# Holding the input loads of later batches until the batch ahead is turned, with a rearranged first batch and a split last tile

## The chip, the cores and the metric

The kernel runs on one core of one Trainium2 chip. The metric is the device time of one execution in microseconds (us), the median over several executions. A profile shows one execution alone: the kernel before took 443.82 us in its profiled run, and its span, from the first to the last of the program's instructions, is 442.0 us. Engines are named as the profile names them: PE is TensorE's matmuls, PEld its weight loads, DVE is VectorE, ACT is ScalarE, POOL is GpSimd, SP is SyncE. A trailing q (SPq) is the engine's queue of instructions that issue transfers.

Two kernels are compared by the ratio of mean times: the mean of one kernel's fast runs over the mean of the other's in the same rounds, so a ratio is not quite the ratio of the medians quoted beside it.

## The reference, cut to what matters

```python
batch, n_q_heads, n_kv_heads, seq, head_dim = (8, 16, 4, 384, 64)

def _attn_ref(q, k, v):                       # grouped-query attention
    k = np.repeat(k, 4, axis=1); v = np.repeat(v, 4, axis=1)
    scores = np.matmul(q, k.transpose(0, 1, 3, 2)) / np.sqrt(64)
    attn = np.exp(scores - scores.max(-1, keepdims=True))
    attn = attn / (attn.sum(-1, keepdims=True) + 1e-09)
    return np.matmul(attn, v)

def _moe_ref(x, w_in, w_out):                 # x: 3072 x 1024
    h = np.maximum(x @ w_in, 0.0)             # 1024 x 2048, "up"
    return h * h @ w_out                      # 2048 x 1024, "down"
```

Inputs and output are float32; the kernel computes in bfloat16.

## The kernel before: the parts that matter

One batch at a time goes through: load k, q, v (GpSimd issues the transfers, which also cast to bfloat16); *turn* k and q, that is transpose them so that the head dimension lies on the partitions; scores; exponential; attention times values; turn the result; up; down; store. Batches 0 and 1 are turned by TensorE. From batch 2 on, three transposing transfers issued by SyncE do it, one for k and one for each half of q.

```python
NST, NEX, NXT, NHR, NY = 2, 8, 3, 4, 3      # two staging buffers for k, q, v

def load_k(b):
    st = b % NST
    R.add("gpsimd", lambda g: g.dma_start(k_st[st]..., k[b]...),
          writes=[("k_st", st)], dma=f"k{st}", cost=1.3, issue=0.8)

def turn_q_dma(b, half):                    # SyncE
    R.add("sync", lambda e: e.dma_start_transpose(out=qT[b % 2][...], in_=q_st[b % NST][...]),
          reads=[("q_st", ...)], writes=[("qT", ...)], dma=f"turn_q{half}", cost=2.5)

# ... cut: at the start, in this order on GpSimd's queue: batch 0, three chunks of w_in,
#     batch 1, five chunks of w_in, four chunks of w_out ...
```

The order of instructions on every engine is fixed when the program is built. A planner keeps a modelled clock for each engine, and at each step appends to TensorE's order the piece of work that its model says is ready. The hardware then runs that order:

```python
while av_q or sc_q or o_q or f_head is not None:
    if loaded + 1 < B and turned >= loaded + 1 - NST and not turn_q:
        loaded += 1
        load_k(loaded)
        load_q(loaded, 0, 8)
        load_q(loaded, 8, 16)
        load_v(loaded)
    # ... cut: queue the turns of the next batch; list what is ready; append one piece to TensorE ...
```

With `turned` starting at 1 and `NST` at 2, the loads of batches 2 and 3 are both issued as soon as batch 1 is turned. In the first batch the kernel before swaps two half tiles:

```python
items = list(ffn(b))
if b == 0:
    items[1], items[2] = items[2], items[1]
```

The softmax here doesn't subtract the row's maximum and nothing guards it: scores larger than these inputs give would overflow.

## Time and profile before

| | before |
|---|---|
| median of 3 runs | 444.37 us (444.08 to 444.77) |
| span of the profile | 442.0 us |
| PE busy | 423.0 us, 96% |
| PE idle in one stall | 77.15 to 86.90 us |

The page of the kernel before: busy times, then three rows of the span in 40 slices of 11.05 us. A digit is tenths busy; PEclk is the granted TensorE clock in tenths.

```profile
PE 423.0 (96%) x3438; PEld 230.2 (52%) x3438; DVE 159.0 (36%) x333; ACT 193.1 (44%) x189; POOL 55.1 (12%) x68
...
PE   7799999199999999999999999999999999999997
...
PEclk9999999699999999999999999999999999999999
DMA  9999999999589359448017220023100110110011
```

PE is full but for the first slices, the last one and one slice that reads 1, at 77 to 88 us. That slice also has the only lowered clock. The transfer engines are full through the first 110 us.

The timeline of the kernel before around that slice. Columns: start, duration, engine, line, operation, out<-in, shape, count; the bracket is the idle time of the engine before it and what ended it.

```profile
64.04 13.11 PE L450 MATMUL ps<-w_out_sb,h2T 128*128 128x512 bf16 x60
...
69.66 3.21 SPq L263 DMA_TRANSPOSE kT<-k_dup  x1
...
72.91 11.62 SPq L269 DMA_TRANSPOSE qT<-q_st  x2
...
86.90 1.46 PE L342 MATMUL ps<-qT,kT 64*128 64x512 bf16 x8 [9.75 <-DMA qT<-q_st]
...
88.30 2.83 PE L450 MATMUL ps<-w_out_sb,h2T 128*128 128x512 bf16 x8
```

PE runs 60 down matmuls of batch 0 to 77.15, then waits 9.75 us for the first query turn of batch 2. Work for PE exists in that time (eight down matmuls, the up matmuls of batch 1), but in the fixed order it stands behind the scores.

The table by stretches of the kernel before. Columns: length and PE busy (count), the same for PEld, DVE, ACT and POOL, then granted clock, transfer share (the packets' summed time over that of 16 engines; it can pass 1, as packets overlap), GB/s.

```profile
75.00:80.00 5.00, 2.15 (x10) 0.78 (x8) 0.69 (x1) 0.00 (x0) 0.28 (x1) 1.00 1.39 178
80.00:85.00 5.00, 0.00 (x0) 0.00 (x0) 0.00 (x0) 0.00 (x0) 0.00 (x0) 0.50 1.39 179
85.00:90.00 5.00, 3.10 (x13) 1.04 (x14) 0.00 (x0) 1.59 (x1) 2.18 (x3) 0.50 1.19 218
```

PE does nothing from 80 to 85, the transfer engines are no less busy, and the clock is at half, so the first work after the wait runs at half speed too.

GpSimd's timeline in the kernel before, the loads of batches 2 and 3 (k, two halves of q, v, twice; the first k of each and the last v are shown), and what waited for the first ones:

```profile
30.84 0.79 POOL L202 DMA_DIRECT2D k_st<-in_k_dram  x1
...
34.07 0.81 POOL L202 DMA_DIRECT2D k_st<-in_k_dram  x1
...
36.55 0.84 POOL L220 DMA_DIRECT2D v_st<-in_v_dram  x1
65.89 1.47 POOL L254 COPY k_dup<-k_st 128x1536 bf16<-128x1536 bf16 x1 [28.49 <-DMA k_st<-in_k_dram]
73.76 0.83 POOL L259 COPY v_aug<-v_st 128x768 bf16<-128x768 bf16 x1 [6.41 <-DMA v_st<-in_v_dram]
```

Batch 2's first piece lands at 65.8 and its last at 73.7, because both weight matrices, 8.4 MB each in float32, are ahead of it in the queue. Batch 3 follows in the same queue; by the trace's record of landings its four pieces land at 76.0, 79.7, 83.4 and 85.3, just while the turns of batch 2 run.

How long the first query turn took from issue to landing, in the kernel before, for batch 2 (issued at 72.91) and for batch 4 (issued at 127.11, nothing loading beside it):

```profile
DMA to landing us min/median/max: 13.9/13.9/13.9
```

```profile
DMA to landing us min/median/max: 3.9/3.9/3.9
```

ScalarE's first chain of exponentials and up work of batch 0, in the kernel before:

```profile
7.28 16.61 ACT L332 ACTIVATE expT<-ps 128x1024 bf16<-128x1024 f32 x18 [4.79 <-PE ps L322]
...
21.52 0.82 PE L422 MATMUL ps<-xT,w_in_sb 128*128 128x384 bf16 x4
...
23.29 0.81 PE L422 MATMUL ps<-xT,w_in_sb 128*128 128x384 bf16 x4
```

The last copy of the kernel before, and (transfers of the last 8 us) the time from issue to landing of the stores there:

```profile
438.85 0.69 DVE L462 COPY y_sb<-ps 128x512 f32<-128x512 f32 x1 [2.76 <-PE ps L450]
```

```profile
out_dram<-y_sb SPq DMA_DIRECT2D x2, 256.0 KB, 2.0
```

### The profile page before, as it was taken

To read this page: it belongs to the slowest core of one execution; us is meant where nothing else is said; L and a number is where in the kernel's file an instruction comes from. 1 tells how busy PE (TensorE), PEld (TensorE's weight loads), DVE (VectorE), ACT (ScalarE), POOL (GpSimd) and SP (SyncE) were. 2 spreads that over 40 slices of the span, in tenths; PEclk is the share of its full clock that TensorE was granted. 3 is DMA by queue.
4 is the path that set the end of the run, shared out by engine and by line. 5 is a ranking of instruction groups with operands and counts; after the bars stand their busy time and mean duration, and the time that the engine had idled before them with its cause. 6 is when DMAs were issued, how large, how long until landed. Compare 5 with 4: busy or idle time off the path is not lost.

```text
span 442.0 us, 7776 instructions
## 1 busy us (share of the span) xinstructions
PE 423.0 (96%) x3438; PEld 230.2 (52%) x3438; DVE 159.0 (36%) x333; ACT 193.1 (44%) x189; POOL 55.1 (12%) x68
## 2 busy tenths in 40 slices
PE   7799999199999999999999999999999999999997
PEld 4465554055644556445564455555565456446543
DVE  4374441034423445223452334343342234124411
ACT  4937730067743676545755457722131023003300
POOL 7763002043022013020000000000000000000000
PEclk9999999699999999999999999999999999999999
DMA  9999999999589359448017220023100110110011
GB/s 148 194 196 203 183 193 213 196 160 171 72 160 192 76 101 139 82 91 165 19 37 150 78 78 19 1 62 99 57 0 25 71 49 0 50 71 25 1 73 71
DMA packets 95187, 43.90 MB, mean 99 GB/s; under 512 B 75696, under 2 KB 89008, under 8 KB 95152
## 3 DMA queue, kind: packets, MB, share of 16 engines
q0 software_dynamic: 36544, 17.44, 31.0%
q1 hardware_dynamic: 58080, 25.57, 26.5%
q8 instruction: 27, 0.44, 0.4%
q10 hardware_dynamic: 528, 0.39, 0.3%
q14 instruction: 8, 0.07, 0.1%
HBM read 35.65 MB, written 12.58 MB: 109 GB/s over the span
## 4 chain that ended last, share of the span: by engine, by line
PE 89%; DMA 4%; ACT 3%; DVE 2%; SPq 1%; issue 0%
PE ps L422 38%; PE ps L450 36%; PE ps L367 7%; PE ps L342 7%; DMA qT<-q_st 3%; ACT expT L332 3%; DMA q_f<-in_q_dram 1%; SPq L263 1%; DVE qT L303 1%; DVE y_sb L462 0%; DVE o_sb L380 0%; DVE kT L287 0%; DVE xT L404 0%; DVE q_st L509 0%; PE ps L322 0%
## 5 line engine op out<-in xcount | busy, mean ns | idle before, releaser
L422 PE MATMUL ps<-xT,w_in_sb 128*128 128x384 bf16 x1024 | 174.1, 326 | 0.0
L450 PE MATMUL ps<-w_out_sb,h2T 128*128 128x512 bf16 x768 | 173.1, 381 | 0.0
L352 ACT ACTIVATE expT<-ps 128x3072 bf16<-128x3072 f32 x42 | 114.4, 2725 | 81.8 <-PE ps L342 81.0
L422 PEld LDWEIGHTS ps<-xT,w_in_sb 128*128 128x128 bf16 x1024 | 97.1, 98 | 69.2 <-issue 5.6
L434 ACT ACTIVATE h2T<-hr 128x384 bf16<-128x384 f32 x128 | 64.4, 521 | 138.4 <-DVE hr L432 138.2
L450 PEld LDWEIGHTS ps<-w_out_sb,h2T 128*128 128x128 bf16 x768 | 72.8, 98 | 89.5 <-issue 7.6
L432 DVE TENSOR_SCALAR hr<-ps 128x384 f32<-128x384 f32 x128 | 71.3, 557 | 103.6 <-PE ps L422 103.6
L462 DVE COPY y_sb<-ps 128x512 f32<-128x512 f32 x48 | 33.2, 692 | 142.3 <-PE ps L450 142.3
L342 PE MATMUL ps<-qT,kT 64*128 64x512 bf16 (+1 forms) x336 | 35.2, 330 | 10.1 <-DMA qT<-q_st 9.7
L367 PEld LDWEIGHTS ps<-v_aug,expT 128*128 128x128 bf16 x1152 | 39.8, 97 | 6.1 <-DVE rinv L374 0.5
L367 PE MATMUL ps<-v_aug,expT 128*128 128x65 bf16 x1152 | 41.3, 193 | 0.0
L380 DVE TENSOR_TENSOR o_sb<-ps,rinv 128x384 bf16<-128x384 f32 x64 | 35.7, 558 | 2.4 <-DVE rinv L374 0.2
L342 PEld LDWEIGHTS ps<-qT,kT 64*128 64x128 bf16 x336 | 13.1, 95 | 31.1 <-DMA qT<-q_st 10.2
L374 DVE RECIPROCAL rinv<-ps 128x6 f32<-128x6 f32 x64 | 12.2, 190 | 25.9 <-PE ps L367 25.9
L227 POOL DMA_DIRECT2D q_st<-in_q_dram x17 | 14.9, 886 | 44.1 <-DMA qT<-q_st 43.4
L259 POOL COPY v_aug<-v_st 128x768 bf16<-128x768 bf16 x8 | 6.7, 832 | 98.2 <-PE ps L367 87.6
L332 ACT ACTIVATE expT<-ps 128x1024 bf16<-128x1024 f32 x18 | 16.6, 1112 | 4.8 <-PE ps L322 4.8
L254 POOL COPY k_dup<-k_st 128x1536 bf16<-128x1536 bf16 x7 | 10.3, 1478 | 31.4 <-DMA k_st<-in_k_dram 31.4
L322 PE MATMUL ps<-qT,kT 64*128 64x512 bf16 (+1 forms) x48 | 6.7, 329 | 3.2 <-ACT expT L332 2.4
L237 POOL DMA_DIRECT2D w_in_sb<-in_moe_w_in_dram x8 | 7.1, 930 | 0.0
L220 POOL DMA_DIRECT2D v_st<-in_v_dram x8 | 6.3, 784 | 0.1
L202 POOL DMA_DIRECT2D k_st<-in_k_dram x7 | 5.4, 765 | 0.0
(25 smaller groups left out, 40.5 us busy)
## 6 DMA issues: line engine op xcount, KB each, us to landing
out_dram<-y_sb SPq DMA_DIRECT2D x48, 256.0 KB, 2.0
q_st<-in_q_dram POOLq DMA_DIRECT2D x14, 384.0 KB, 8.3
w_in_sb<-in_moe_w_in_dram POOLq DMA_DIRECT2D x8, 512.0 KB, 16.0
w_out_sb<-in_moe_w_out_dram POOLq DMA_DIRECT2D x4, 1024.0 KB, 26.5
v_st<-in_v_dram POOLq DMA_DIRECT2D x8, 192.0 KB, 10.1
k_st<-in_k_dram POOLq DMA_DIRECT2D x7, 192.0 KB, 10.5
q_st<-in_q_dram POOLq DMA_DIRECT2D x3, 192.0 KB, 5.0
xT<-o_sb SPq DMA_TRANSPOSE x28, 2.8
```

What stands on the lines that cost most here:

```text
L227: R.add("gpsimd", lambda g: g.dma_start(q_st[st][:, h0:h1, :], q[b, h0:h1].rearrange("h (p j) d -> p h (j d)", j=NJ)), writes=[("q_st", st ...
L332: R.add("scalar", lambda e: e.activation(dst, src, AF.Exp, scale=0.125), reads=keys, writes=[("expT", (n + m) % NEX, c0 // 512) for m in r ...
L342: m = pe.matmul(flat[:, k0 * HC + c0:k0 * HC + c1], kT[b % 2][64 * x:64 * x + 64, u + k0, :], q_cols(b, (u + k0) // NJ, x, c0, c1))
L352: R.add("scalar", lambda e: e.activation(dst, src, AF.Exp, scale=0.125), reads=keys, writes=[("expT", (n + m) % NEX, h) for m in range(2) ...
L367: m = pe.matmul(po[:, f - 6 * s2, 0:D + 1], w, v_aug[b % 2][:, g * NJ + j, 0:D + 1], start=(j == 0), stop=(j == NJ - 1))
L374: R.add("vector", lambda e: e.reciprocal(rinv[r].ap().unsqueeze(2), po[:, :, D:D + 1]), reads=[("bank", i)], writes=[("rinv", r)], cost=0.13)
L380: R.add("vector", lambda e: e.tensor_tensor(dst, srcv, rbv, ALU.mult), reads=[("bank", i), ("rinv", r)], writes=[("o_sb", o, s2)], cost=0.48)
L422: m = pe.matmul(bank(i)[:, 0:S], w_in_sb[:, kc, c * 128:(c + 1) * 128], xT[b % NXT][:, kc, :], start=(kc == 0), stop=(kc == NKC - 1))
L432: R.add("vector", lambda e: e.tensor_scalar_max(hr[r][:, :], bank(i)[:, 0:S], 0.0), reads=[("bank", i)], writes=[("hr", r)], cost=0.48)
L434: R.add("scalar", lambda e: e.activation(h2T[b % 2][:, c, :], hr[r][:, :], AF.Square), reads=[("hr", r)], writes=[("h2T", b % 2, c)], cost ...
L450: m = pe.matmul(bank(i), h2T[b % 2][:, c, i3 * 128:(i3 + 1) * 128], w_out_sb[:, c, jj * 512:(jj + 1) * 512], start=(c == 0), stop=(c == NF ...
L462: R.add("vector", lambda e: e.tensor_copy(ysl, bank(i)), reads=[("bank", i)], writes=[("y", yb)], cost=0.61)
```

## The change

The intent has three parts. **(1)** Loads of batch 3 and later wait until the batch ahead is turned, so that no load competes with a turn. **(2)** The first batch: the first query group is loaded ahead of three quarters of the keys; its cast and its turn are split so that scores can begin sooner; two up tiles are opened in quarters while ScalarE is the limit; attention-times-value goes out in halves; scores use two pairs of PSUM banks in place of three, which frees banks 6 and 7 for the up tiles. **(3)** The last down tile is split into 384 and 128 columns, so that less is left to copy and store after the last matmul.

```diff
-    def load_k(b):
+    def load_k(b, after=()):
...
-            writes=[("k_st", st)], dma=f"k{st}", cost=1.3, issue=0.8)
+            reads=after, writes=[("k_st", st)], dma=f"k{st}", cost=1.3, issue=0.8)
...
-        if loaded + 1 < B and turned >= loaded + 1 - NST and not turn_q:
+        if loaded + 1 < B and turned >= loaded and not turn_q:
             loaded += 1
-            load_k(loaded)
+            after = [("qT", (loaded - 1) % 2, HKV - 1, 1)] if loaded > 2 else []
+            load_k(loaded, after)
... (2) the first batch, cut to its core ...
+        keys("sync", 0, 1)
         R.add("scalar", lambda e: e.dma_start(q_f32[:, :, :], ...))
+        keys("scalar", 1, HKV)
...
+    R.add("vector", lambda e: e.tensor_copy(q_to[:, 0:512], q_from[:, 0:512]), ...)
+    R.add("scalar", lambda e: e.copy(q_to[:, 512:768], q_from[:, 512:768]), ...)
...
-                t = max(R.when(reads=reads), R.when(writes=[("bank", 2 * (u % 3) + i) for i in range(2)]))
+                t = max(R.when(reads=reads), R.when(writes=[("bank", 2 * (u % 2) + i) for i in range(2)]))
...
-            if b == 0:
-                items[1], items[2] = items[2], items[1]
+        opened = 2 if b == 0 else 0
+        for k0 in range(0, NKC, 2):
+            for c in range(opened):
+                yield up_part(b, c, ats[c], k0, k0 + 2)
... (3) the last tile ...
+                last = b == B - 1 and (jj, i3) == (1, NJ - 1)
+                for c0, c1 in ((512, 896), (896, 1024)) if last else ((512 * jj, 512 * jj + 512),):
```

The rest of the diff splits the bookkeeping keys of q into two parts and moves nested functions out; it adds no other work.

More of the change, by code (lines that the diff above doesn't have):

```diff
@@ L204, in load_k, with keys @@
             k[b].rearrange("g (p j) d -> p g (j d)", j=NJ)),
-            writes=[("k_st", st)], dma=f"k{st}", cost=1.3, issue=0.8)
+            reads=after, writes=[("k_st", st)], dma=f"k{st}", cost=1.3, issue=0.8)
     def first_loads():
-        for g0, g1 in ((0, 1), (1, HKV)):
-            R.add("sync", lambda e, g0=g0, g1=g1: e.dma_start(
+        def keys(eng, g0, g1):
+            R.add(eng, lambda e: e.dma_start(
                 k_f32[:, g0 * NJ:g1 * NJ, :].rearrange("p (g j) d -> p g (j d)", j=NJ),
                 k[0, g0:g1].rearrange("g (p j) d -> p g (j d)", j=NJ)),
-                writes=[("k_f32", g) for g in range(g0, g1)], dma=f"kf{g0}", cost=0.4 * (g1 - g0), issue=0.3)
+                writes=[("k_f32", g) for g in range(g0, g1)], dma=f"kf{g0}", cost=0.4 * (g1 - g0), issue=0.4)
+        keys("sync", 0, 1)
         R.add("scalar", lambda e: e.dma_start(
             q_f32[:, :, :], q[0, 0:4].rearrange("h (p j) d -> p h (j d)", j=NJ)),
-            writes=["q_f32"], dma="qf", cost=1.3, issue=0.3)
+            writes=["q_f32"], dma="qf", cost=1.3, issue=0.4)
+        keys("scalar", 1, HKV)
     def load_v(b):
@@ L229, in load_q @@
             q[b, h0:h1].rearrange("h (p j) d -> p h (j d)", j=NJ)),
-            writes=[("q_st", st, h // 4) for h in range(h0, h1, 4)], dma=f"q{st}_{h0}",
+            writes=[("q_st", st, h // 4, x) for h in range(h0, h1, 4) for x in range(2)], dma=f"q{st}_{h0}",
             cost=0.33 * (h1 - h0), issue=0.8)
@@ L271, in turn_q_dma @@
             in_=q_st[b % NST][:, 8 * half:8 * half + 8, :].rearrange("p h e -> p (h e)")),
-            reads=[("q_st", b % NST, 2 * half + i) for i in range(2)],
-            writes=[("qT", b % 2, 2 * half + i) for i in range(2)], dma=f"turn_q{half}", cost=2.5)
+            reads=[("q_st", b % NST, 2 * half + i, x) for i in range(2) for x in range(2)],
+            writes=[("qT", b % 2, 2 * half + i, x) for i in range(2) for x in range(2)], dma=f"turn_q{half}", cost=2.5)
     def turn_k_pe(b, g, banks):
@@ L288, in turn_k_pe, with turn_q_pe @@
               reads=[("bank", i)], writes=[("kT", b % 2, g)], cost=0.27)
-    def turn_q_pe(b, g, banks):
+    def turn_q_pe(b, g, banks, t0=0, t1=6):
         i = pick(banks)
@@ L293, in turn_q_pe, with score_reads @@
         src = q_st[b % NST][:, 4 * g:4 * g + 4, :].rearrange("p h e -> p (h e)")
+        parts = [h for h in range(2) if t0 < (4, 6)[h] and t1 > (0, 4)[h]]
         def tr(pe):
-            for t in range(6):
-                m = pe.matmul(pt[:, t * 128:(t + 1) * 128], src[:, t * 128:(t + 1) * 128], ident[:],
+            for t in range(t0, t1):
+                m = pe.matmul(pt[:, (t - t0) * 128:(t - t0 + 1) * 128], src[:, t * 128:(t + 1) * 128], ident[:],
                               is_transpose=True)
             return m
-        R.add("tensor", tr, reads=[("q_st", b % NST, g), "ident"], writes=[("bank", i)], cost=0.36)
-        dst = qT[b % 2][:, 6 * g:6 * g + 6, :].rearrange("p n c -> p (n c)")
-        R.add("vector", lambda e: e.tensor_copy(dst, pt[:, 0:768]),
-              reads=[("bank", i)], writes=[("qT", b % 2, g)], cost=0.47)
-    def score_reads(b, u):
+        R.add("tensor", tr, reads=[("q_st", b % NST, g, h) for h in parts] + ["ident"], writes=[("bank", i)],
+              cost=0.06 * (t1 - t0))
+        dst = qT[b % 2][:, 6 * g + t0:6 * g + t1, :].rearrange("p n c -> p (n c)")
+        R.add("vector", lambda e: e.tensor_copy(dst, pt[:, 0:(t1 - t0) * 128]),
+              reads=[("bank", i)], writes=[("qT", b % 2, g, h) for h in parts], cost=0.07 + 0.068 * (t1 - t0))
+    def score_reads(b, u, parts=(0, 1)):
         g = u // NJ
-        return [("kT", b % 2, g), ("qT", b % 2, g)]
+        return [("kT", b % 2, g)] + [("qT", b % 2, g, h) for h in parts]
     def q_cols(b, g, x, c0, c1):
@@ L326, in burst_small @@
         keys = [("bank", base), ("bank", base + 1)]
-        R.add("tensor", sc, reads=[r for u, _ in pieces for r in score_reads(b, u)], writes=keys,
+        R.add("tensor", sc, reads=[r for u, c0 in pieces for r in score_reads(b, u, (c0 // 512,))], writes=keys,
               cost=0.22 + 0.19)
@@ L361, in av, with mm @@
         po = bank(i)[:, 0:2 * NJ * DP].rearrange("p (f e) -> p f e", f=2 * NJ)
-        def mm(pe):
-            for f in range(6 * s2, 6 * s2 + 6):
+        def mm(pe, f0):
+            for f in range(f0, f0 + NJ):
                 for j in range(NJ):
@@ L369, in mm @@
             return m
-        R.add("tensor", mm, reads=av_reads(b, g), writes=[("bank", i)], cost=0.58)
+        R.add("tensor", lambda pe: mm(pe, 6 * s2), reads=av_reads(b, g), writes=[("bank", i)], cost=0.285)
+        yield
+        R.add("tensor", lambda pe: mm(pe, 6 * s2 + 3), reads=av_reads(b, g), writes=[("bank", i)], cost=0.285)
         r = (b * 8 + c) % 2
@@ L409, in bass_gqa_attention__then__ffn_squared_relu_kernel @@
     y_n = [0]
-    def ffn(b):
-        for c in range(NFC):
-            at = []
-            for half in range(2):
-                def piece(c=c, half=half, at=at):
-                    if half == 0:
-                        at.append(pick((6, 7)))
-                    i = at[0]
-                    def mm(pe):
-                        for kc in range(4 * half, 4 * half + 4):
-                            m = pe.matmul(bank(i)[:, 0:S], w_in_sb[:, kc, c * 128:(c + 1) * 128],
-                                          xT[b % NXT][:, kc, :], start=(kc == 0), stop=(kc == NKC - 1))
-                        return m
-                    R.add("tensor", mm, reads=[("w_in", c * 128 // WC)] +
-                          [("xT", b % NXT, kc) for kc in range(4 * half, 4 * half + 4)],
-                          writes=[("bank", i)], cost=0.65)
-                    if half == 1:
-                        r = hr_n[0] % NHR
-                        hr_n[0] += 1
-                        R.add("vector", lambda e: e.tensor_scalar_max(hr[r][:, :], bank(i)[:, 0:S], 0.0),
-                              reads=[("bank", i)], writes=[("hr", r)], cost=0.48)
-                        R.add("scalar", lambda e: e.activation(h2T[b % 2][:, c, :], hr[r][:, :], AF.Square),
-                              reads=[("hr", r)], writes=[("h2T", b % 2, c)], cost=0.42)
-                need = [("w_in", c * 128 // WC)] + [("xT", b % NXT, kc) for kc in range(4 * half, 4 * half + 4)]
-                yield need, (6, 7) if half == 0 else None, piece
@@ new lines, in up_part, with piece, mm @@
+    def up_part(b, c, at, k0, k1):
+        def piece():
+            if k0 == 0:
+                at.append(pick((6, 7)))
+            i = at[0]
+            def mm(pe):
+                for kc in range(k0, k1):
+                    m = pe.matmul(bank(i)[:, 0:S], w_in_sb[:, kc, c * 128:(c + 1) * 128],
+                                  xT[b % NXT][:, kc, :], start=(kc == 0), stop=(kc == NKC - 1))
+                return m
+            R.add("tensor", mm, reads=need, writes=[("bank", i)], cost=0.1625 * (k1 - k0))
+            if k1 == NKC:
+                r = hr_n[0] % NHR
+                hr_n[0] += 1
+                R.add("vector", lambda e: e.tensor_scalar_max(hr[r][:, :], bank(i)[:, 0:S], 0.0),
+                      reads=[("bank", i)], writes=[("hr", r)], cost=0.48)
+                R.add("scalar", lambda e: e.activation(h2T[b % 2][:, c, :], hr[r][:, :], AF.Square),
+                      reads=[("hr", r)], writes=[("h2T", b % 2, c)], cost=0.42)
+        need = [("w_in", c * 128 // WC)] + [("xT", b % NXT, kc) for kc in range(k0, k1)]
+        return k1, need, (6, 7) if k0 == 0 else None, piece
@@ L439, in ffn @@
+    def ffn(b):
+        opened = 2 if b == 0 else 0
+        ats = [[] for _ in range(opened)]
+        for k0 in range(0, NKC, 2):
+            for c in range(opened):
+                yield up_part(b, c, ats[c], k0, k0 + 2)
+        for c in range(opened, NFC):
+            at = []
+            for k0 in (0, 4):
+                yield up_part(b, c, at, k0, k0 + 4)
         for jj in range(2):
             for i3 in range(NJ):
-                at = []
-                for part in range(4):
-                    def piece(jj=jj, i3=i3, part=part, at=at):
-                        if part == 0:
-                            at.append(pick((6, 7)))
-                        i = at[0]
-                        def mm(pe):
-                            for c in range(4 * part, 4 * part + 4):
-                                m = pe.matmul(bank(i), h2T[b % 2][:, c, i3 * 128:(i3 + 1) * 128],
-                                              w_out_sb[:, c, jj * 512:(jj + 1) * 512],
-                                              start=(c == 0), stop=(c == NFC - 1))
-                            return m
-                        R.add("tensor", mm, reads=[("w_out", jj, part // 2)] +
-                              [("h2T", b % 2, c) for c in range(4 * part, 4 * part + 4)],
-                              writes=[("bank", i)], cost=0.865)
-                        if part == 3:
-                            yb = y_n[0] % (2 * NY)
-                            y_n[0] += 1
-                            ysl = y_sb[yb // 2][:, (yb % 2) * 512:(yb % 2) * 512 + 512]
-                            R.add("vector", lambda e: e.tensor_copy(ysl, bank(i)),
-                                  reads=[("bank", i)], writes=[("y", yb)], cost=0.61)
-                            rows = out[b * S:(b + 1) * S, :].rearrange("(p j) f -> j p f", j=NJ)[i3]
-                            R.add("sync", lambda e: e.dma_start(rows[:, jj * 512:(jj + 1) * 512], ysl),
-                                  reads=[("y", yb)], writes=[("out", b, i3, jj)], dma=f"y{yb}", cost=1.0)
-                    need = [("w_out", jj, part // 2)] + [("h2T", b % 2, c) for c in range(4 * part, 4 * part + 4)]
-                    yield need, (6, 7) if part == 0 else None, piece
@@ new lines, in ffn, with down_part, piece, mm @@
+                last = b == B - 1 and (jj, i3) == (1, NJ - 1)
+                for c0, c1 in ((512, 896), (896, 1024)) if last else ((512 * jj, 512 * jj + 512),):
+                    at = []
+                    for part in range(4):
+                        yield down_part(b, jj, i3, c0, c1, part, at)
+    def down_part(b, jj, i3, c0, c1, part, at):
+        n = c1 - c0
+        def piece():
+            if part == 0:
+                at.append(pick((6, 7)))
+            i = at[0]
+            def mm(pe):
+                for c in range(4 * part, 4 * part + 4):
+                    m = pe.matmul(bank(i)[:, 0:n], h2T[b % 2][:, c, i3 * 128:(i3 + 1) * 128],
+                                  w_out_sb[:, c, c0:c1], start=(c == 0), stop=(c == NFC - 1))
+                return m
+            R.add("tensor", mm, reads=need, writes=[("bank", i)], cost=4 * (n / 2400 + 0.0025))
+            if part == 3:
+                yb = y_n[0] % (2 * NY)
+                y_n[0] += 1
+                ysl = y_sb[yb // 2][:, (yb % 2) * 512:(yb % 2) * 512 + n]
+                R.add("vector", lambda e: e.tensor_copy(ysl, bank(i)[:, 0:n]),
+                      reads=[("bank", i)], writes=[("y", yb)], cost=0.08 + n / 960)
+                rows = out[b * S:(b + 1) * S, :].rearrange("(p j) f -> j p f", j=NJ)[i3]
+                R.add("sync", lambda e: e.dma_start(rows[:, c0:c1], ysl),
+                      reads=[("y", yb)], writes=[("out", b, i3, c0)], dma=f"y{yb}", cost=1.0)
+                stored.append(("out", b, i3, c0))
+        need = [("w_out", jj, part // 2)] + [("h2T", b % 2, c) for c in range(4 * part, 4 * part + 4)]
+        return 0, need, (6, 7) if part == 0 else None, piece
@@ L472, in bass_gqa_attention__then__ffn_squared_relu_kernel @@
+    stored = []
     R.add("vector", lambda e: e.memset(warm[:], 0.0), writes=["warm"])
@@ L508, in bass_gqa_attention__then__ffn_squared_relu_kernel @@
     dup_k(0, "vector", 0, 1)
-    R.add("vector", lambda e: e.tensor_copy(q_st[0][:, 0:4, :], q_f32[:, :, :]),
-          reads=["q_f32"], writes=[("q_st", 0, 0)], cost=0.5)
-    ALL, LOW, HIGH = tuple(range(8)), tuple(range(6)), (6, 7)
+    q_to = q_st[0][:, 0:4, :].rearrange("p h e -> p (h e)")
+    q_from = q_f32.ap().rearrange("p h e -> p (h e)")
+    R.add("vector", lambda e: e.tensor_copy(q_to[:, 0:512], q_from[:, 0:512]),
+          reads=["q_f32"], writes=[("q_st", 0, 0, 0)], cost=0.6)
+    R.add("scalar", lambda e: e.copy(q_to[:, 512:768], q_from[:, 512:768]),
+          reads=["q_f32"], writes=[("q_st", 0, 0, 1)], cost=0.4)
+    LOW, MID, HIGH = tuple(range(6)), (4, 5), (6, 7)
     smalls = []
@@ L518, in bass_gqa_attention__then__ffn_squared_relu_kernel @@
             smalls.append([(u - 1, 512), (u, 512)])
-    turn_q = [(b, g, w) for b in range(2) for g in range(HKV) for w in "kq"]
+    turn_q = [(0, 0, "k"), (0, 0, "a"), (0, 0, "c")]
+    turn_q += [(b, g, w) for b in range(2) for g in range(HKV) for w in "kq" if (b, g) != (0, 0)]
     sc_q = [(0, n) for n in range(len(smalls))] + [(b, u) for b in range(1, B) for u in range(0, NU, 2)]
@@ L533, in prepare @@
         for half in range(2):
-            chores.append(([("q_st", b % NST, 2 * half)], lambda half=half: turn_q_dma(b, half)))
+            chores.append(([("q_st", b % NST, 2 * half, 0)], lambda half=half: turn_q_dma(b, half)))
         chores.append(([("v_st", b % NST)], lambda: aug_v(b, "gpsimd")))
@@ L538, in feed @@
         for b in range(B):
-            items = list(ffn(b))
-            if b == 0:
-                items[1], items[2] = items[2], items[1]
-            for n, item in enumerate(items):
-                yield (b, n) + item
+            for item in ffn(b):
+                yield (b,) + item
     def open_bank(banks):
@@ L549, in bass_gqa_attention__then__ffn_squared_relu_kernel @@
     f_head = next(feeding)
+    av_open = None
     margin = 0.5
-    while av_q or sc_q or o_q or f_head is not None:
+    while av_q or av_open or sc_q or o_q or f_head is not None:
         now = R.clock["tensor"]
         first = bool(sc_q) and sc_q[0][0] == 0
-        spare = HIGH if first else LOW
-        if loaded + 1 < B and turned >= loaded + 1 - NST and not turn_q:
+        spare = MID if first else LOW
+        if loaded + 1 < B and turned >= loaded and not turn_q:
             loaded += 1
-            load_k(loaded)
+            after = [("qT", (loaded - 1) % 2, HKV - 1, 1)] if loaded > 2 else []
+            load_k(loaded, after)
             load_q(loaded, 0, 8)
@@ L570, in bass_gqa_attention__then__ffn_squared_relu_kernel @@
             b, g, w = turn_q[0]
-            src = [("k_dup", b, g)] if w == "k" else [("q_st", b, g)]
+            src = [("k_dup", b, g)] if w == "k" else [("q_st", b, g, h) for h in range(2) if w != "ac"[1 - h]]
             cand.append((max(R.when(reads=src), open_bank(spare)), 1, "turn"))
-        if av_q:
+        if av_open is not None:
+            cand.append((now, 2, "av2"))
+        elif av_q:
             b, c = av_q[0]
@@ L582, in bass_gqa_attention__then__ffn_squared_relu_kernel @@
                 top = max(p[0] for p in smalls[u])
-                ok = ("q", 0, top // NJ) in turned_g and pairs // 2 * NJ + NEX >= top + 1
-                reads = [r for p in smalls[u] for r in score_reads(0, p[0])]
-                t = max(R.when(reads=reads), R.when(writes=[("bank", 2 * (u % 3) + i) for i in range(2)]))
+                ok = all((0, p[0] // NJ, p[1] // 512) in turned_g for p in smalls[u])
+                ok = ok and pairs // 2 * NJ + NEX >= top + 1
+                reads = [r for p in smalls[u] for r in score_reads(0, p[0], (p[1] // 512,))]
+                t = max(R.when(reads=reads), R.when(writes=[("bank", 2 * (u % 2) + i) for i in range(2)]))
                 if ok:
@@ L588, in bass_gqa_attention__then__ffn_squared_relu_kernel @@
             else:
-                ok = (("q", b, (u + 1) // NJ) in turned_g) if b == 1 else turned >= b
+                ok = ((b, (u + 1) // NJ, 1) in turned_g) if b == 1 else turned >= b
                 t = max(R.when(reads=score_reads(b, u) + score_reads(b, u + 1)),
@@ L594, in bass_gqa_attention__then__ffn_squared_relu_kernel @@
         if f_head is not None:
-            b, n, need, banks, piece = f_head
-            if x_done[b] >= 8 or (x_done[b] >= 4 and not first and b == 0 and n < 2):
+            b, chunks, need, banks, piece = f_head
+            if x_done[b] >= chunks:
                 t = R.when(reads=need)
@@ L609, in bass_gqa_attention__then__ffn_squared_relu_kernel @@
             b, g, w = turn_q.pop(0)
-            (turn_k_pe if w == "k" else turn_q_pe)(b, g, spare)
-            turned_g.add((w, b, g))
+            if w == "k":
+                turn_k_pe(b, g, spare)
+            else:
+                turn_q_pe(b, g, spare, *dict(q=(0, 6), a=(0, 4), c=(4, 6))[w])
+            turned_g |= {(b, g, h) for h in range(2) if w in ("q", "ac"[h])}
         elif what[2] == "av":
             b, c = av_q.pop(0)
-            av(b, c, spare)
+            av_open = (b, c, av(b, c, spare))
+            next(av_open[2])
+        elif what[2] == "av2":
+            b, c, rest = av_open
+            av_open = None
+            next(rest, None)
             pairs += 1
@@ L627, in bass_gqa_attention__then__ffn_squared_relu_kernel @@
             if b == 0:
-                burst_small(0, smalls[u], 2 * (u % 3))
+                burst_small(0, smalls[u], 2 * (u % 2))
                 halves |= {(p[0], p[1] // 512) for p in smalls[u]}
@@ L635, in bass_gqa_attention__then__ffn_squared_relu_kernel @@
         else:
-            piece()
-            if n == 2 * NFC - 1:
-                up_done = b
+            f_head[4]()
             f_head = next(feeding, None)
-    R.add("sync", lambda e: e.nop(), reads=[("out", b, i, jj) for b in range(B) for i in range(NJ) for jj in range(2)])
+            if f_head is None or f_head[1] == 0:
+                up_done = b if f_head is None else f_head[0]
+    R.add("sync", lambda e: e.nop(), reads=stored)
     R.emit()
```

## The prediction

> **What bounds the kernel.** TensorE: PE is busy 423.0 of 442.0 us (page) and 89% of the chain of waits. Only idle or slow-clocked time can be won; the timeline shows where:
>
> - One stall in batch 0's down projection. PE runs dry at 77.15 us and waits 9.75 us for "DMA qT<-q_st" (list of waits); batch 2's scores start at 86.90. The table by stretches grants clock 0.50 from 80 to about 90: the 8 score matmuls take 1.46 us (0.76 elsewhere), the next 8 down matmuls 2.77 (1.73). From 86.90 to the second score burst at 92.43 is 5.53 us; warm, 0.76 + 1.73 + 1.30 = 3.79. Cost: 9.75 + 1.74 = 11.5 us.
> - The first 30 us: start-up, and 18 small exponentials (ScalarE, 7.28 to 23.89) with PE partly idle.
> - The end: last matmul near 438.8, a 0.69 us copy, a store, 442.0.
>
> **Why the stall.** Loads of batches 2 and 3 are issued together (30.84 to 37.4), behind the weights. By the trace's landings, batch 2 is in by 73.7 (first half of its queries at 68.6), batch 3 by 85.3, used after 120. The key turn, issued at 69.66, lands at 80.5; the first query turn, issued at 72.91, at 86.9: 13.9 us, against 3.9 where nothing loads (127.11 to 131.0). The Trainium skill, "DMA: Bandwidth & Descriptors", section "Queues, rings and completion order", says that each DMA engine alternates between queues packet by packet; a turn slowed 3.6 times agrees.
>
> **What the change does.**
> 1. Load 3 on waits for the second query turn of the batch before. Nothing competes after about 73.7, when the key turn is half done. Estimate, from the uncontended 3.9 us and about 1.8 us between successive turns: first query turn lands at about 77.3 (76 to 79.5). Later batches have tens of us of slack (load 10 us, turns 6): no new stall.
> 2. First group: q ahead of three quarters of k; cast (0.91 us) and turn copy (0.56) split: first exponential 0.6 us sooner. Two up tiles opened early fill PE gaps. PE reaches the stall point 1.5 to 2 us sooner, about 75.5; but DMA sets the resume, so this mostly turns into waiting.
> 3. Last tile as 384 + 128: last copy about 0.25 us instead of 0.69, so 0.45 us. Matmul work unchanged.
> 4. Attention-times-value in halves: nothing beyond batch 0.
>
> **Sum.** Stall about 1.8 us (0 to 3.5), short enough for the clock to stay up (before, it fell 2.85 us after the last matmul; the skill's "TensorE: Matmul & The Clock Gate", section "Why this matters for your kernels", warns of gaps over about 3 us). Second burst at 77.3 + 3.8 = 81.1 instead of 92.43: 11.3 us. With the tail about 11.7: 444.4 becomes **432.8 us**, range 430.8 to 436.0. Faster by over 2% (under 435.5) 0.83; within 2% 0.16; slower 0.01.
>
> **Right if:** wait for qT<-q_st under 3.5 us; batch 2's first query turn lands in 4 to 6 us; clock 1.0 from 75 to 90; batch 3's loads issued after about 79; first exponential near 6.7; tail copy 0.25 us; PE busy down about 1.7 us.
>
> **Wrong if:** load 2 or the turns themselves slow the turn: resume near 80, clock drops, 435 to 437. Resume before 76: the first-batch gain counts, 431. A held load arrives late enough to stall batch 3 or 4. Two score bank pairs instead of three leave gaps in ScalarE's first chain.

## More of the kernel before

The trace also has each packet of the transfers. Queue, packets, MB and share of the engines, in the kernel before from 75 to 84 us (`--dma --window`); q0 is GpSimd's queue with the loads (packets of 384 bytes), q1 SyncE's with the turns (256 bytes):

```profile
q0 software_dynamic: 2542, 0.96, 85.2%
q1 hardware_dynamic: 2543, 0.64, 54.1%
```

The counts are equal: the two queues advance packet for packet, and the turns get 283 packets per us.

## The result, and the profile after

The changed kernel took 431.61 us (431.35 to 432.37, 4 runs) against 444.51 us (444.08 to 444.77, 4 runs); the ratio is 0.9714, 95% interval 0.9697 to 0.9730. Two repeats on other occasions gave 0.9731 and 0.9740. Executions over 1.5% slower than the fastest of the same kernel are left out of the means. The forecast was 432.8 us, range 430.8 to 436.0.

| | before | after |
|---|---|---|
| median | 444.51 us | 431.61 us |
| span of the profile | 442.0 us | 430.6 us |
| PE reaches the stall point | 77.15 us | 77.42 us |
| PE waits there | 9.75 us | 0.45 us |
| second score burst of batch 2 starts | 92.43 us | 81.83 us |
| end of the span minus that | 349.6 us | 348.8 us |

The page of the changed kernel, same lines:

```profile
PE 421.8 (98%) x3428; PEld 231.6 (54%) x3454; DVE 158.9 (37%) x335; ACT 194.0 (45%) x190; POOL 55.6 (13%) x68
...
PE   8899999999999999999999999999999999999997
```

The slice that read 1 now reads 9; PE's idle share went from 4% to 2%.

The timeline of the changed kernel around the former stall (line numbers moved: L471 is the down matmul, L347 the score, L266 and L272 the turns):

```profile
66.25 11.17 PE L471 MATMUL ps<-w_out_sb,h2T 128*128 128x512 bf16 x50
...
69.92 3.54 SPq L266 DMA_TRANSPOSE kT<-k_dup  x1
...
73.50 3.86 SPq L272 DMA_TRANSPOSE qT<-q_st  x2
...
77.87 0.82 PE L347 MATMUL ps<-qT,kT 64*128 64x512 bf16 x8 [0.45 <-DMA qT<-q_st]
...
78.63 1.90 PE L471 MATMUL ps<-w_out_sb,h2T 128*128 128x512 bf16 x8
...
80.10 0.74 POOL L202 DMA_DIRECT2D k_st<-in_k_dram  x1 [5.15 <-DMA qT<-q_st]
```

The key turn and the query turns are issued at nearly the same times as before, 69.92 and 73.50. What changed is that they land: the pair takes 3.86 us to issue in place of 11.62, PE waits 0.45 us, and its score matmuls take 0.82 us in place of 1.46. The last line is batch 3's first load, held until the second query turn has landed.

(The program has 52 down matmuls before these scores; this trace lacks two of the records, other traces of the same order show 52.)

The table by stretches, the landing of the first query turn of batch 2, and SyncE's queue from 75 to 77 us, when no load is beside the turns, in the changed kernel:

```profile
75.00:80.00 5.00, 4.49 (x26) 1.86 (x25) 0.69 (x1) 1.26 (x1) 0.00 (x0) 1.00 1.12 255
80.00:85.00 5.00, 5.00 (x35) 2.64 (x34) 1.80 (x3) 4.01 (x3) 4.20 (x5) 1.00 0.87 160
...
```

```profile
DMA to landing us min/median/max: 4.3/4.3/4.3
```

```profile
q1 hardware_dynamic: 2168, 0.55, 128.0%
```

That is 1084 packets of the turns per us, 3.8 times the rate beside the loads. The clock column needs care: the trace of this execution holds no clock record at all, and the view then reads 1.00. What shows full speed here is the 0.82 us of the eight score matmuls.

ScalarE's first chain and the early up work of the changed kernel:

```profile
6.94 3.08 ACT L337 ACTIVATE expT<-ps 128x1024 bf16<-128x1024 f32 x3 [1.85 <-PE ps L327]
...
10.33 14.10 ACT L337 ACTIVATE expT<-ps 128x1024 bf16<-128x1024 f32 x15 [0.30 <-PE ps L327]
...
19.65 0.49 PE L426 MATMUL ps<-xT,w_in_sb 128*128 128x384 bf16 x2
...
20.39 0.50 PE L426 MATMUL ps<-xT,w_in_sb 128*128 128x384 bf16 x2
...
21.15 0.82 PE L426 MATMUL ps<-xT,w_in_sb 128*128 128x384 bf16 x4
```

The chain starts 0.34 us sooner but has gaps, and ends at 24.43 in place of 23.89. The early up work is eight matmuls, as it was before.

The tail of the changed kernel: the last copies, and the stores of the last 7 us with their time to landing.

```profile
427.39 0.56 DVE L480 COPY y_sb<-ps 128x384 f32<-128x384 f32 x1 [1.91 <-PE ps L471]
428.28 0.29 DVE L480 COPY y_sb<-ps 128x128 f32<-128x128 f32 x1 [0.34 <-PE ps L471]
```

```profile
out_dram<-y_sb SPq DMA_DIRECT2D x1, 64.0 KB, 1.5
```

### The profile page after: what moved, and what is told of

Same layout as the page of the kernel before. It is cut to its first block, busy times and chain, and to the rows that moved or that the text cites. A ratio compares the mean times of both kernels' runs of the same rounds, so it can differ in the third digit from the quotient of the medians.

```text
span 430.6 us, 7790 instructions
## 1 busy us (share of the span) xinstructions
PE 421.8 (98%) x3428; PEld 231.6 (54%) x3454; DVE 158.9 (37%) x335; ACT 194.0 (45%) x190; POOL 55.6 (13%) x68
## 4 chain that ended last, share of the span: by engine, by line
PE 92%; ACT 3%; DMA 2%; DVE 1%; SPq 1%; issue 1%
PE ps L426 39%; PE ps L471 37%; PE ps L347 7%; PE ps L372 7%; ACT expT L337 3%; DMA qT<-q_st 1%; DMA q_f<-in_q_dram 1%; PE ps L301 1%; SPq L266 1%; DVE o_sb L387 1%; PE ps L327 0%; PE ps L285 0%; DVE qT L308 0%; DVE y_sb L480 0%; DVE rinv L381 0%
## 5 line engine op out<-in xcount | busy, mean ns | idle before, releaser
L471 PE MATMUL ps<-w_out_sb,h2T 128*128 128x512 bf16 (+2 forms) x758 | 167.7, 375 | 1.7 <-issue 0.5
L471 PEld LDWEIGHTS ps<-w_out_sb,h2T 128*128 128x128 bf16 x784 | 73.6, 98 | 87.9 <-issue 6.0
L480 DVE COPY y_sb<-ps 128x512 f32<-128x512 f32 (+2 forms) x49 | 33.3, 681 | 130.7 <-PE ps L471 130.7
L347 PE MATMUL ps<-qT,kT 64*128 64x512 bf16 (+1 forms) x336 | 34.6, 325 | 0.5 <-DMA qT<-q_st 0.5
L347 PEld LDWEIGHTS ps<-qT,kT 64*128 64x128 bf16 x336 | 13.0, 94 | 21.2 <-DVE o_sb L387 4.9
```

The costliest lines, as they stand in the source:

```text
L347: m = pe.matmul(flat[:, k0 * HC + c0:k0 * HC + c1], kT[b % 2][64 * x:64 * x + 64, u + k0, :], q_cols(b, (u + k0) // NJ, x, c0, c1))
L471: m = pe.matmul(bank(i)[:, 0:n], h2T[b % 2][:, c, i3 * 128:(i3 + 1) * 128], w_out_sb[:, c, c0:c1], start=(c == 0), stop=(c == NFC - 1))
L480: R.add("vector", lambda e: e.tensor_copy(ysl, bank(i)[:, 0:n]), reads=[("bank", i)], writes=[("y", yb)], cost=0.08 + n / 960)
```

## The experiments

The theory to test, called C in the expectations: the bytes of load 3, sharing the transfer engines with the turns of batch 2, were the stall, and taking them away is nearly all of the gain. Rivals: F, the new first batch or the new order carries a good part; O, load 3 did harm by its place in GpSimd's order or its semaphores, not by its traffic. Twelve runs were made in three groups of four (two of the twelve are the changed kernel again). The first two groups ran on one chip, the third on another; each group has its own executions of the kernel before. All results were correct.

### The hold alone, and everything but the hold

Edit of the first, on the kernel before: the hold lines of the diff above and nothing else. TensorE's order is unchanged instruction for instruction. Edit of the second, on the changed kernel:

```diff
-        if loaded + 1 < B and turned >= loaded and not turn_q:
+        if loaded + 1 < B and turned >= loaded + 1 - NST and not turn_q:
-            after = [("qT", (loaded - 1) % 2, HKV - 1, 1)] if loaded > 2 else []
+            after = []
```

Expected of the hold alone:

> The kernel before with part 1 of the change alone: loads of batch 3 on wait for the second query turn of the batch ahead. TensorE's order is that of the kernel before, instruction for instruction. Theory C (the competing bytes of load 3 were the stall, and the hold is nearly all of the gain): the first query turn of batch 2 lands within 4 to 6 us of its issue, PE waits under 1.5 us for it, clock stays at 1.0, and the time is 432.4 us (431.9 to 433.0), that is the changed kernel plus 0.8 us for its tail. Rival F (the new first batch or the new order on SyncE carries a good part of the gain): 435 us or more.

Measured: 433.34 us (433.13 to 433.74) against 443.69; ratio 0.9761 (0.9740 to 0.9782). Its list of waits:

```profile
PE ps L342 <- DMA qT<-q_st: 0.5, 1, 0.5
```

Expected of everything but the hold:

> The changed kernel with only the hold undone; TensorE's order is that of the changed kernel. Theory C: the stall comes back whole, first query turn 12 to 15 us from issue to landing, clock 0.5 for about 10 us, time 443.7 us (443.0 to 444.3), so that everything else in the change is worth about 0.8 us, the tail. Rival F: 441 us or less.

Measured: 443.50 us (442.47 to 444.34); ratio 0.9987 (0.9967 to 1.0007). Its list of waits:

```profile
PE ps L347 <- DMA qT<-q_st: 9.6, 1, 9.6
```

The clock fell to 0.5 for 10.24 us again, by the trace's clock records. So the hold alone gives almost the whole gain (10.6 us by the means, where the changed kernel gained 11.9 on the same chip) and the rest without the hold almost none. F falls. The hold alone came in 0.3 us above its expected range: on this chip the changed kernel took 432.31 us (mean, below), and the tail and the first batch, 0.8 and 0.3 us, make up the difference.

### The decoy: the bytes without the dependence

Edit, on the changed kernel: right behind batch 2's loads, four more with the shapes and bytes of load 3, into tiles that nothing reads (two dead ones and two new ones). The orders of TensorE, ScalarE, VectorE and SyncE are those of the changed kernel.

```diff
             load_v(loaded)
+            if loaded == 2:
+                decoy()        # k[3], q[3, 0:8], q[3, 8:16], v[3] into unread tiles
```

> The changed kernel, with four loads added right behind batch 2's on the same queue: the bytes, shapes and places in the queue of the old load 3, but into tiles that nothing reads. Nothing waits for them, and TensorE, ScalarE, VectorE and SyncE keep the order of the changed kernel. Theory C: the bytes alone bring the stall back: first query turn 12 to 15 us, resume at 86 to 88, clock 0.5, time 442.5 to 444.5 us. Rival O (the old load did harm through its place among GpSimd's instructions or through its semaphores, not through its traffic): 431.6 us, at most 433.

Measured: 442.25 us (440.86 to 442.44); ratio 0.9956 (0.9935 to 0.9977). Timeline, then the first query turn's landing:

```profile
72.72 11.15 SPq L287 DMA_TRANSPOSE qT<-q_st  x2
...
85.34 1.46 PE L362 MATMUL ps<-qT,kT 64*128 64x512 bf16 x8 [8.79 <-DMA qT<-q_st]
```

```profile
DMA to landing us min/median/max: 12.6/12.6/12.6
```

The stall is back, with its slow issue, its wait and its half-speed scores, and nothing was added but loads that no engine waits for. O falls. The time is 0.25 us below the expected range; the real load 3 was followed by batch 4's keys, which the decoy was not, and that may be the difference.

### Half of the decoy

Edit: only the decoy's first two loads (keys and half of the queries).

> The decoy cut to its first two loads (keys and half of the queries), half of the bytes. Theory C: the turn is done a couple of us after the loads' traffic ends; half the bytes push that from 74 to about 79.5, first query turn lands at 80 to 82.5, wait of 3 to 5.5 us, the clock may or may not drop, time 434.5 to 438. If any load behind the turn does the same harm whatever its size (a fixed cost of a busy queue): as the full decoy, 442.

Measured: 437.89 us (436.72 to 438.73); ratio 0.9867 (0.9845 to 0.9890). List of waits and landing:

```profile
PE ps L360 <- DMA qT<-q_st: 4.6, 1, 4.6
```

```profile
DMA to landing us min/median/max: 8.5/8.5/8.5
```

Half of the bytes do about half of the harm (4.6 us of waiting against 8.8), and the clock was down for 6.83 us in place of 10.24. By the trace's landings the four kernels line up:

| kernel | last load beside the turn lands | first query turn lands |
|---|---|---|
| changed | 74.1 us | 77.8 us |
| half decoy | 79.3 us | 81.0 us |
| full decoy | 85.1 us | 85.3 us |
| everything but the hold | 84.4 us (batch 4's keys 86.4) | 86.6 us |

In these four the first query turn landed 0.2 to 3.8 us after the last load beside it. That is no rule for every turn: the key turn, which goes first, landed at 80.5 in the kernel before, ahead of the last load at 85.3. The two kernels with decoys ran on different chips, so "half" is rough.

### The last tile whole, and the first batch of before

Edit of the first, on the changed kernel: the split condition taken out. The second is the kernel before with the hold and the split tile, so it differs from the changed kernel by the first batch alone. The changed kernel ran again beside it.

```diff
-                for c0, c1 in ((512, 896), (896, 1024)) if last else ((512 * jj, 512 * jj + 512),):
+                for c0, c1 in ((512 * jj, 512 * jj + 512),):
```

Expected of the whole tile:

> The changed kernel with the last tile whole. If the tail is worth what the prediction put (the copy alone, 0.45 us): 432.05 us. If the smaller last store also lands sooner, as the two profiles suggest (2.06 us against 1.53 from the end of the copy to its landing): 0.8 us, 432.4 us.

Measured: 433.13 us (432.89 to 433.39); ratio 0.9755 (0.9734 to 0.9776). Both expected times are missed, by 0.7 us and more: they started from 431.6 us for the changed kernel, which took 432.3 on this chip. The difference between the two kernels is what counts, below.

Expected of the changed kernel again:

> The changed kernel unaltered, for comparison on the same chip and rounds as the next three. Ratio to the kernel before as on record, 0.970 to 0.973; the wait for the query turn of batch 2 between 0.4 and 1.0 us.

Measured: 432.06 us (431.70 to 432.97); ratio 0.9731 (0.9705 to 0.9758). Its profile shows no wait for that turn at all, a miss of the lower bound: batch 2 had landed by 72.5 and the turn by 76.6, and TensorE came to it at 77.55.

Expected of hold and tail:

> The kernel before with the hold and the split last tile, but with its own first batch. Reading of the traces so far: the new first batch brings TensorE to the stall point only 0.0 to 0.7 us sooner, and the resume is set by DMA anyway, so this kernel equals the changed one within 0.4 us. If the new first batch is worth the 1.5 us or more that the prediction gave it and is not hidden, this kernel is over 1 us slower. The split tile: 0.8 us faster than the hold alone.

Measured: 432.58 us (432.23 to 433.14); ratio 0.9737 (0.9712 to 0.9762).

The two groups ran on the same chip, and give each part twice. The tail, from whole tile to changed: means 433.13 and 432.31, 0.8 us; from the hold alone to hold and tail: means 433.39 and 432.63, 0.8 us. (By the ratios both are 0.24%, 1.1 us.) The first batch, from hold and tail to changed: 0.3 us; from the hold alone to whole tile: 0.3 us. The intervals of all these ratios overlap, and the tail's two differences are between groups that ran at different times; its 0.8 us has a second source, the profiles (below). The first batch's 0.3 us, twice the same, is a direction rather than a size.

### Batch 2 sooner: the last weight chunk behind half of its queries

If transfers set the resume, moving batch 2 ahead of a weight chunk should remove the rest of the wait.

```diff
-    for jj in range(2):
-        for part in range(2):
-            load_w_out(jj, part)
+    for jj, part in ((0, 0), (0, 1), (1, 0)):
+        load_w_out(jj, part)
...
             load_q(loaded, 0, 8)
+            if loaded == 2:
+                load_w_out(1, 1)
             load_q(loaded, 8, 16)
```

> The changed kernel with the last chunk of the second weight matrix loaded between the two query halves of batch 2, so that batch 2's keys and first half of queries land some 6 us sooner. If the resume at 77.9 us is set by DMA, as the prediction said, the rest of the wait (0.45 to 0.7 us) goes, TensorE goes straight into batch 2's scores, and the time falls by 0.3 to 0.8 us against the changed kernel. If the remaining wait is something else (the order on SyncE, TensorE itself), the time stays.

Measured: 436.61 us (435.23 to 437.29); ratio 0.9824 (0.9799 to 0.9849). Slower than the changed kernel by over 4 us: a miss. Its timeline:

```profile
65.17 7.07 PE L471 MATMUL ps<-w_out_sb,h2T 128*128 128x512 bf16 x32
...
68.39 5.56 SPq L272 DMA_TRANSPOSE qT<-q_st  x1
...
76.00 1.02 PE L347 MATMUL ps<-qT,kT 64*128 64x512 bf16 x8 [3.76 <-DMA qT<-q_st]
```

The turn did land sooner, at 76.0 us, though it took 7.6 us, for the rest of batch 2 (landed at 72.2 and 74.1) now came beside it, and the weight chunk (67.5) beside the key turn ahead of it. But the planner, whose model gives a turn the same time in any traffic, saw batch 2 ready sooner and put the scores behind 32 down matmuls where the changed kernel has 52. TensorE got there 20 matmuls early and waited 3.76 us, with the clock down for 3.41 us.

A second kernel added a fix to the first batch: the load of the third query group is modelled 1.2 us later, so the fourth score burst goes ahead of that group's turn.

```diff
-    load_q(0, 8, 12)
+    load_q(0, 8, 12, 1.2)      # late: added to the modelled cost
```

> The previous kernel, and in the first batch the fourth score burst goes ahead of the turn of the third query group, whose load lands at 8.5 to 9.2 us and stands in TensorE's order in front of that burst. Reading: that wait left gaps of 0.3 to 0.7 us in ScalarE's first chain of exponentials in three of four profiles. Expected: no gap, first chain ends at 23.5 instead of 24.1 to 24.4, a further 0.3 to 0.7 us. Rival: the chain is held up elsewhere and nothing is gained.

Measured: 435.85 us (435.65 to 436.30); ratio 0.9811 (0.9786 to 0.9836). Its first chain, with no gap, ends at 23.27:

```profile
6.54 16.73 ACT L337 ACTIVATE expT<-ps 128x1024 bf16<-128x1024 f32 x18 [1.57 <-PE ps L327]
```

It is 0.8 us under its neighbour in the median and 0.6 us in the mean, as expected, but the neighbour's chain also ran without a gap in its one profile (6.50 to 23.57), so the gap is not shown to be the reason.

### The same with TensorE's order kept

Edit, on the previous kernel, whose first-batch fix stays in:

```diff
     # turn_q_dma
+        if b == 2:
+            R.ops[-1]["end"] += 4.5      # the model alone: scores stay behind 52 matmuls
```

> The previous kernel (last weight chunk between the two query halves of batch 2, first-batch fix), but with TensorE's order of the changed kernel kept: there the first score burst of batch 2 stands behind 52 down matmuls, in the two reordered kernels behind 32 and 32. Reading of those two: the turn did land sooner (75.8 against 77.8 us), but the planner had moved the burst 20 matmuls forward, so TensorE stood before it 3.8 us with work left. Expected here: turn at about 75.8, TensorE there at 76.3 to 77.2, no wait, 0.5 to 1.1 us faster than the changed kernel. Rival (the loads' new order itself costs the 4 us, through the second weight matrix or the values coming late): 435 us or more again.

Measured: 430.66 us over all five runs, 430.48 to 430.91 in four; ratio 0.9709 (0.9692 to 0.9727). The changed kernel, in the same rounds:

> The changed kernel once more, on this chip, for comparison with the other three: 431.3 to 432.3.

Measured: 431.89 us, 431.67 to 432.61 in four runs; ratio 0.9740 (0.9722 to 0.9758). The means of the fast runs are 430.65 and 432.01, 1.4 us apart, more than the expected 0.5 to 1.1; the first-batch fix is part of it, and how much was not measured apart.

### Three dummy matmuls more before the first scores

Edit, on the previous kernel: two dummy matmuls after the first key turn and one after the first query turn.

> The first kernel of this group with three more dummy matmuls in TensorE's gaps before the first scores (two after the first key turn, one after the first query turn). Reading: in two of seven profiles of the new first batch the matmuls took twice as long up to 9.5 us, and the first exponential started at 6.9 to 7.3 instead of 6.5. If it is the short idle gaps that keep the clock down, the first exponential starts by 6.65 and the spread of the runs narrows; at most 0.3 us in the median. If not: no difference, or 0.1 us slower.

Measured: 430.70 us (430.49 to 430.91); ratio 0.9711 (0.9694 to 0.9728). No difference from the kernel without them, and its first exponential started at 6.90, which misses the 6.65: the cast of the queries ran later in this run (4.83). Whether the dummies keep the clock up stays open. Its timeline at the former stall shows what the previous kernel was built for:

```profile
65.31 11.17 PE L473 MATMUL ps<-w_out_sb,h2T 128*128 128x512 bf16 x50
...
76.42 0.82 PE L349 MATMUL ps<-qT,kT 64*128 64x512 bf16 x8
```

There is no bracket behind the score matmuls: PE goes straight on, at 76.42, as the first query turn has landed at 75.8. So the reordered loads were sound, and the 4 us lost before were the moved burst: with the order of TensorE put back, by the model alone, they are gone.

## Why the prediction was right

The time and its main mechanism held, point by point:

- **The stall and its cost.** Put at 11.5 us with the slowed work after it; the hold alone took 10.6 us off (means 444.0 and 433.4). The decoy shows that the competing bytes made it, and half of the decoy that the harm follows their amount.
- **The turn.** Put at 77.3 us (76 to 79.5); landed at 77.8, 4.3 us after issue. Round-robin between the queues, which the Trainium skill describes in "DMA: Bandwidth & Descriptors", section "Queues, rings and completion order", is what the packet counts show: 2,542 of the loads and 2,543 of SyncE's queue in the same 9 us, and 3.8 times as many per us for the turns once the loads are in. It fits the landings, 12.6 us after issue with the full decoy and 8.5 with half.
- **The clock.** It stayed up through the short wait. The profile of the changed kernel shows this by its matmuls only (no clock record); the one with the last tile whole has records, and they give 1.0 from 4.40 to 431.07 us, across a wait of 0.69 us. The skill's "TensorE: Matmul & The Clock Gate", section "What's actually happening", gives a free-running window of 3413 ns. The lowered stretches here were 10.24 us (before, no hold, full decoy), 6.83 (half decoy) and 3.41 or 3.42 (the two reordered kernels), which are three, two and one such window. From the last matmul to the fall it was 2.7 to 5.2 us in these six profiles, so the 2.85 us of the prediction is one case and no limit to plan by; in the two reordered kernels the clock fell 0.5 and 1.3 us after PE had resumed.
- **No new stall.** The loads of batches 3 to 7, issued later, made PE wait nowhere in the changed kernel's list of waits.

Two terms of the sum were mis-sized, in opposite directions:

- **"PE reaches the stall point 1.5 to 2 us sooner, about 75.5."** It reached it at 77.42 in this profile. Over six profiles with the new first batch and this order it came at 76.5 to 77.6 (mean 77.0), and over three with the old one at 77.2 to 77.3: 0.2 us. The step that failed is "Two up tiles opened early fill PE gaps". The kernel before had opened two up tiles as well, in halves, and the timelines show eight early matmuls in both kernels. The other gain of this part, the sooner first exponential (6.5 us in four profiles, 6.9 and 7.3 in two where the first matmuls ran slow), was partly lost again: with two bank pairs, TensorE stood at the turn of the third query group while ScalarE ran out, 0.60 us in the profile without the hold, for example. Such gaps are the last point under "Wrong if" of the prediction, and they came. That the lost bank pair made them was not tested alone: TensorE stood there for the load of that group, and three of the six profiles of this first batch show no gap. As PE came later, the wait was 0.45 us and not 1.8; as the turn still landed last, the total barely felt it. This was in part luck: the margin was under 1 us in the four profiles with the hold where PE waited (0.45 to 0.91), and in the fifth, the changed kernel run again, PE itself came last.
- **"Last copy about 0.25 us instead of 0.69, so 0.45 us."** The copy went from 0.69 to 0.29, but the last store is also a quarter the size and landed 1.5 us after its issue in place of 2.0. The tail was worth 0.8 us in the pair of profiles and 0.8 in both pairs of kernels.

The sum in the profiles: 10.6 us up to the second burst of batch 2 (predicted 11.3) and 0.8 after it (predicted 0.45), 11.4 against a predicted 11.7. That the two errors nearly cancel is luck. The times gained more, 12.7 us by the means of that occasion and 11.9 and 11.7 on the two others: the profile before was of an execution 0.7 us under its median, the one after 0.8 us over. Where executions of one kernel differ was not looked into. PE's busy time fell by 1.2 us (predicted 1.7), with ten fewer matmuls recorded, so it is not a close check.

## What to carry to other kernels

A load that is not needed yet is not free while a transfer in small packets (256 bytes here) on the critical path shares the transfer engines: hold it until that transfer has landed, and check with a decoy that sends the same bytes to nowhere. When engine orders are fixed by a model, bringing data sooner can make things slower, because the model moves the consumer as well; keep the order fixed while testing a reordering of loads. Before crediting a change with opening work early, count in the trace how much of that work the kernel before had already opened.

## What the Trainium skill lacked or had wrong

- "DMA: Bandwidth & Descriptors" gives no time for a transposing transfer within SBUF beside bulk loads. Here the same query turn, always behind a key turn, took 3.9 us with no load beside it, 8.5 and 12.6 us beside half and all of a batch's load, and its issue on SyncE (two of them) grew from 3.86 to 11.62 us.
- "DMA: Bandwidth & Descriptors", section "Anatomy of one DMA", puts a near constant fixed cost of about 2.0 us on a DMA issued by GpSimd. For stores issued by SyncE it has a time to the first byte, but none of that kind, to the landing; the last store of 64 KB landed 1.5 us after issue, one of 256 KB after 2.0.
- "TensorE: Matmul & The Clock Gate", section "What's actually happening", says that the warm-up depends on where the window falls. No page gives how far that reaches with gaps: after 14 dummy matmuls (1.05 to 4.22 us), eight profiles record the rise of the clock at 3.8 to 5.4 us, but four (the changed kernel twice, the hold alone, hold and tail) still ran matmuls at about half rate up to 9.5 us and later (in the changed kernel four score matmuls took 1.04 us, 0.61 where the clock was up). The traces of these four hold no clock record, so the view's 1.00 is no measurement there.
- No page reports a whole execution slowed like the one of 1113.68 us (a single run of the changed kernel; its others on that chip took 431.67 to 432.61). Its trace has no clock record either; PE was busy for 1098.3 us in place of 421.8, VectorE for 163.9 and ScalarE for 200.0, near their 158.9 and 194.0, so TensorE alone was slow. Why stays open.
